# Decode attention: V loads moved from ACT's queue to SP's, with semaphores shared to make room

## The chip, the cores and the metric

The kernel runs on one core of a Trainium2 chip. The metric is the device time of one execution in microseconds (us). The core has five engines that run side by side, each with its own instruction stream: PE (matrix products; PEld is its loading of the stationary operand), DVE (vector), ACT (activations), POOL and SP. Sixteen DMA engines move data between HBM and the on-chip memory SBUF; an engine's instruction starts a transfer, and the transfer then runs by itself. PSUM is the memory into which PE writes its products.

The engines know of each other through semaphores only: an instruction, or a transfer when it lands, raises a semaphore, and an engine waits until it has reached a value. Raising by a transfer is by 16.

## What is computed

One token is decoded for two sequences. There are 32 heads of 128 values; the cache of each sequence and head holds 8192 keys and as many values. All of K and V (64 blocks of 2 MB each) is read once.

```python
xn = _layernorm(x)                                   # x: [2, 1, 512]
q  = (xn @ wq) as [2, 32 heads, 1, 128]
scores = einsum("bhqd,bhkd->bhqk", q, k_cache) * 128 ** -0.5   # k_cache: [2, 32, 8192, 128]
p  = softmax(scores)
o  = einsum("bhqk,bhkd->bhqd", p, v_cache)
return x + o.reshape(2, 1, 4096) @ wo + relu(xn @ w1) @ w2
```

Data is bf16. The program reads 280.5 MB from HBM, nearly all of it K and V.

## The kernel before

**Pairs.** The 64 blocks (sequence and head) are taken two at a time: 32 pairs. Partitions 0 to 63 hold one block of the pair and 64 to 127 the other. A pair's K is one tile of 128 x 16384 bf16, 4 MB, and so is its V. There are two buffers for K (`ks`) and two for V (`vs`), `R = 2`, used in turn. So K of pair t + 2 may be loaded once the K of pair t has been used, and V of pair t + 1 once the V of pair t - 1 has been used.

**One step of PE.** For every pair PE runs `step`. It waits for K of the pair (`dK`), then goes through 16 groups of 8 slices: group e is transposed into a PSUM tile (`transposes`, line 286), copied by DVE or ACT into SBUF (`kcopy`, line 413; the groups of `ON_ACT` go to ACT, the others to DVE), and multiplied with q (`scores`, line 293), two groups behind the transposes. Then come the products of the *preceding* pair's weights with its V (`weighted`, line 306): PE waits for V in `values` only here, more than half way into the step. In between, DVE finds the maximum (lines 467 and 472) and ACT makes the exponentials (line 530). At the end of the step the result is copied out by ACT in `out_copy` (line 518).

So step n uses K of pair n - 1 from its start, and V of pair n - 2 from its second half.

**Semaphores of the groups.** Each group has one for "transposed" (`pT[e]`) and one for "copied" (`kR[e]`), 16 of each; each rises by one in every pair, and the engines wait for the number of the pair, n, which they hold in a register and count up by one.

**Who issues the loads.** SP issues the start (wq into the second V buffer, w1, w2, K of pairs 0 and 1, V of pair 0), and then each K of pair t + 2 when the last group of pair t has been transposed (line 161, after a wait for `pT[NG - 1]`). ACT issues V of pair t + 1 at the end of its own work on pair t (line 548), after `out_copy`, which has waited for `sW`, the end of the products with V of pair t - 1. The two engines have a DMA queue each: in the profile q1 is SP's and q10 ACT's.

**The end.** V of the last pair is loaded by SP in two halves (line 183) when its buffer is free, and after it wo in five pieces (line 188: 14, 7, 6, 3 and 2 of 32 slices) into the place where w1 and w2 were. After the last step PE sums the denominators (line 361) and adds the other branch (line 364), does the products of the last pair with the two halves of V (line 306 again, 128 products), brings the result into the layout that wo needs (lines 379 and 384, with copies of DVE between), and multiplies by wo (line 398, 128 products), waiting for each piece of wo as it comes to it. Two copies, a transpose and the store (line 190) end the program.

**ACT's loop.** ACT's pairs run in a loop of 15 turns of two pairs, and the last two pairs are written out behind it, because no V is issued there.

Of the kernel before, what the change touches and what calls it, by code (L numbers as in the profile page):

```python
# [11 lines left out]
R = 2  # L12
EG = 8
NG = 16
REP = 32
ON_ACT = (0, 3, 5, 8, 11, 13)


@with_exitstack
def kernel(  # L20
# [12 lines left out]
    nc = tc.nc  # L33
    P = 128
# [12 lines left out]
    NP = N // 2  # L47
# [21 lines left out]
    def sem(name):  # L69
        return tc.alloc_semaphore(name)  # L70
# [58 lines left out]
    dW2 = sem("dW2")  # L129
    dK = [sem(f"dK{i}") for i in range(R)]  # L130
    dV = [sem(f"dV{i}") for i in range(R)]
    dH = [sem(f"dH{i}") for i in range(2)]
    dW = [sem(f"dWo{i}") for i in range(5)]
    sG, sI, sQ, sQ1 = sem("sG"), sem("sI"), sem("sQ"), sem("sQ1")
    sV, sA, sE = sem("sV"), sem("sA"), sem("sE")
    sS, sT, sB, sW = sem("sS"), sem("sT"), sem("sB"), sem("sW")
    pT = [sem(f"pT{e}") for e in range(NG)]
    kR = [sem(f"kR{e}") for e in range(NG)]
    sM, sX, sP, sO, sN = sem("sM"), sem("sX"), sem("sP"), sem("sO"), sem("sN")
    sH, sF, sZ = sem("sH"), sem("sF"), sem("sZ")  # L140

# [3 lines left out]
    wo_v = A_wo.rearrange("(p j) n -> p j n", j=WJ)  # L145
    cuts = (0, 14, 21, 27, 30, WJ)
    NC = len(cuts) - 1
    qp = ot[0][0:QG * Bsz, :]
    tpq = tp[1][:].rearrange("p g k -> p (g k)")[:, 0:N].rearrange(
        "p (l c) -> p l c", l=QH  # L150
# [9 lines left out]
    def load_k(t):  # L160
        nc.sync.dma_start(ks[t % R][:], K_all[t * P:(t + 1) * P, :]).then_inc(dK[t % R], 16)

    def load_v(t):
        nc.sync.dma_start(vs[t % R][:], V_all[t * P:(t + 1) * P, :]).then_inc(dV[t % R], 16)
# [5 lines left out]
    @(lambda f: f(nc.sync))  # L170
    def _(sp):
        sp.dma_start(w1_sb, B_w1.rearrange("(p kt) f -> p kt f", kt=KT)).then_inc(dW1, 16)  # L172
        sp.dma_start(w2_sb, B_w2.rearrange("(p j) n -> p j n", j=FJ)).then_inc(dW2, 16)  # L173
        load_k(0)
        load_k(1)
        load_v(0)
        for t in range(NP - 2):
            sp.wait_ge(pT[NG - 1], t + 1)
            load_k(t + R)
        sp.wait_ge(sW, NP - 1)  # L180
        for i in range(2):
            sl = slice(i * SLOT // 2, (i + 1) * SLOT // 2)
            sp.dma_start(
                vs[(NP - 1) % R][:, sl], V_all[(NP - 1) * P:NP * P, sl]
            ).then_inc(dH[i], 16)
        for c in range(NC):
            sl = slice(cuts[c], cuts[c + 1])
            sp.dma_start(wo_sb[:, sl, :], wo_v[:, sl, :]).then_inc(dW[c], 16)
        sp.wait_ge(sE, 1)
        sp.dma_start(  # L190
            out.rearrange("b s (c p) -> (b s c) p", p=P), osb[:]
        ).then_inc(dO, 16)


    @(lambda f: f(nc.gpsimd))
    def _(g):
# [34 lines left out]
    def _(pe):  # L231
# [51 lines left out]
        def transposes(r, e):  # L283
            for i in range(EG):
                kk = e * EG + i
                t = pe.transpose(tp[e % 4][:, i, :], ks[r][:, kk * Dh:(kk + 1) * Dh], identb[:])  # L286
            t.then_inc(pT[e], 1)

        def scores(r, e, n):
            pe.wait_ge(kR[e], n)  # L290
            for i in range(EG):
                kk = e * EG + i
                t = pe.matmul(  # L293
                    Sc[r][:, 2 * kk:2 * kk + 2 * REP],
                    lhsT=kT[e % 4][:, i, :],
                    rhs=rep(q2[r][:]),
                    start=True,
                    stop=True,
                )
            if e == NG - 1:  # L300
                t.then_inc(sS, 1)
# [17 lines left out]
            pe.wait_ge(sO, n)  # L319
            pe.wait_ge(dV[r], n16)  # L320

        def step(r, n, n16):


            pe.wait_ge(dK[r], n16)
            pe.wait_ge(sQ1, n)
            for e in range(NG):
                transposes(r, e)
                if e >= 2:
                    scores(r, e - 2, n)  # L330
            v = 1 - r
            values(v, n, n16)
            weighted(v, 0)
            scores(r, NG - 2, n)
            weighted(v, 1)
            scores(r, NG - 1, n)
            for e in range(2, NG):
                weighted(v, e)
                if e == 5:
                    pe.wait_ge(sM, n)  # L340
                    pe.transpose(tr_of(r), mcol[r][:], identb[:]).then_inc(sT, 1)  # L341
                if e == 8:
                    pe.wait_ge(sX, n)
                    pe.matmul(  # L344
                        bc_of(r), lhsT=onesb[:], rhs=mx[r][:], start=True, stop=True
                    ).then_inc(sB, 1)

        reg = nc.alloc_register(mybir.EngineType.PE, "pairno")
        pe.reg_mov(reg, 0)
        with pe.Fori(16, 16 * (NP // R) + 1, 16) as n16:  # L350
            for r in range(R):
                pe.reg_add(reg, reg, 1)
                step(r, reg, n16)

        pe.wait_ge(sP, NP + 1)
        pe.wait_ge(sO, NP + 1)
# [12 lines left out]
                stop=False,  # L369
            )  # L370
        for i in range(2):
            pe.wait_ge(dH[i], 16)
            for e in range(i * NG // 2, (i + 1) * NG // 2):
                weighted(1, e)

# [16 lines left out]

        pe.wait_ge(sV, 105)
        for c in range(NC):
            pe.wait_ge(dW[c], 16)
            for j in range(cuts[c], cuts[c + 1]):
                for k in range(KT):
                    t = pe.matmul(  # L398
                        fin[:, k, :],
                        lhsT=wo_sb[:, j, k * P:(k + 1) * P],  # L400
                        rhs=OX[:, j, :],
                        start=False,
                        stop=(j == WJ - 1 and k == KT - 1),
                    )
# [3 lines left out]
            tp[1][0:Bsz * KT, 0, :], yT[:].rearrange("p b c -> p (b c)"), identb[:]  # L408
        ).then_inc(sH, 1)

    def kcopy(eng, e):
        fn = eng.copy if e in ON_ACT else eng.tensor_copy
        fn(kT[e % 4][:], tp[e % 4][:]).then_inc(kR[e], 1)  # L413


    @(lambda f: f(nc.vector))
    def _(v):
# [38 lines left out]
        v.wait_ge(sF, 3)  # L456
        v.tensor_tensor(out=ys[:], in0=y, in1=xsb[:], op=ALU.add).then_inc(sF, 1)

        def pair(i, n):
            for e in range(NG):  # L460
                if e not in ON_ACT:
                    v.wait_ge(pT[e], n)
                    kcopy(v, e)
            v.wait_ge(sS, n)
            for u in range(2):
                half = slice(u * HP, (u + 1) * HP)
                m = v.tensor_reduce(  # L467
                    out=mcol[i][half, :], in_=S_of(i)[half, :, u], axis=AX.X, op=ALU.max
                )
            m.then_inc(sM, 1)  # L470
            v.wait_ge(sT, n)
            v.tensor_reduce(  # L472
                out=mx[i][:], in_=tr_of(i).rearrange("o (u m) -> o u m", u=2),
                axis=AX.X, op=ALU.max, negate=True,
            ).then_inc(sX, 1)

        reg = nc.alloc_register(mybir.EngineType.DVE, "pairno_v")
        v.reg_mov(reg, 0)
        with v.Fori(0, NP // R):
            for r in range(R):  # L480
                v.reg_add(reg, reg, 1)
                pair(r, reg)

        v.wait_ge(sH, 1)
        v.reciprocal(out=RD[:], in_=Sc[0][:, 0:N]).then_inc(sV, 1)
# [22 lines left out]
    @(lambda f: f(nc.scalar))  # L508
    def _(a):
        a.wait_ge(sV, 3)  # L510
        a.activation(
            out=rstd[:], in_=mv[:, 1:2], func=ACTF.Sqrt, bias=eps_t[:Bsz], scale=1.0
        ).then_inc(sA, 1)


        def out_copy(r, n, c):
            a.wait_ge(sW, n)
            a.copy(OTf[:, bass.ds(c, 2)], ot[r][:, 0:2]).then_inc(sO, 1)  # L518

        def pair(i, n, t):  # L520
            for e in range(NG):
                if e in ON_ACT:
                    a.wait_ge(pT[e], n)
                    kcopy(a, e)
            a.wait_ge(sB, n)
            a.copy(nm[i][:], bc_of(i)).then_inc(sN, 1)  # L526
            a.wait_ge(sN, n)
            for u in range(2):
                half = slice(u * HP, (u + 1) * HP)
                x = a.activation(  # L530
                    out=prm[i][half, :, u],
                    in_=S_of(i)[half, :, u],
                    func=ACTF.Exp,
                    bias=nm[i][half, u:u + 1],
                    scale=1.0,
                    accum_out=RS[half, bass.ds(t, 1)],
                )
            x.then_inc(sP, 1)
            out_copy(1 - i, n, t * 2)

        a.copy(nm[0][:, 0:1], eps_t[:]).then_inc(sO, 1)
        reg = nc.alloc_register(mybir.EngineType.Activation, "pairno_a")
        a.reg_mov(reg, 0)
        with a.Fori(0, NP // R - 1) as tr:
            for r in range(R):
                a.reg_add(reg, reg, 1)
                pair(r, reg, tr * R + r)
                a.dma_start(  # L548
                    vs[1 - r][:], V_all[bass.ds((tr * R + r + 1) * P, P), :]
                ).then_inc(dV[1 - r], 16)  # L550
        for r in range(R):
            a.reg_add(reg, reg, 1)
            pair(r, reg, NP - R + r)
# [1 line left out]
_INS = ['A_x', 'A_k_cache', 'A_v_cache', 'A_wq', 'A_wo', 'B_x', 'B_w1', 'B_w2']  # L555
_OUTS = [((2, 1, 512), 'bfloat16')]
# [25 lines left out]
```

## Time and profile before

| what | value |
| --- | --- |
| time, median of 3 runs | 665.18 us (665.15 to 665.19) |
| the profiled execution's own time | 665.18 us |
| its span, first to last instruction | 663.1 us |
| PE busy | 562.3 us (85%) |
| DVE busy | 253.3 us (38%) |
| ACT busy | 254.5 us (38%) |
| read from HBM | 280.50 MB, 423 GB/s over the span |
| mean granted clock of PE | 0.941 |

The span is what the profile shows; 2.1 us of the time lie around it. All rows below are of this one execution, and times in them count from the start of the span.

How rows are read. A group or timeline row names start or total in us, the line of the kernel, the engine, the operation, what it writes and reads, and how often. In brackets at the end of a timeline row is how long the engine was idle before it and what released it. SPq and ACTq are the parts of SP and ACT that issue transfers; a row of theirs is the issue, not the transfer. The list of DMA issues has the size of one and the median time from issue to landing. In rows for stretches of time there are the start and end, the length, the busy time of each engine, the granted clock, the mean busy share of the DMA engines and the rate in GB/s.

### The profile page before, as it was taken

How to read it: one execution, taken by the hardware profiler on the slowest of the kernel's cores; microseconds unless marked ns; L12 is line 12 of the kernel's file. 1: busy time of each engine (PE TensorE's matmuls, PEld its weight loads, DVE VectorE, ACT ScalarE, POOL GpSimd, SP SyncE). 2: the span in 40 equal slices, each digit the busy share in tenths (PEclk: the TensorE clock that was granted, in tenths of full speed). 3: DMA queues.
4: the chain of work that ended last, by engine and by line, in shares of the span. 5: the costliest groups of instructions: out<-in, count | busy, mean ns of one | idle time of the engine just before them, and what ended most of it. 6: DMA issues, size and time to landing. Idle time of an engine off the chain costs nothing.

```text
span 663.1 us, 26912 instructions
## 1 busy us (share of the span) xinstructions
PE 562.3 (85%) x12737; PEld 538.2 (81%) x12737; DVE 253.3 (38%) x436; ACT 254.5 (38%) x402; POOL 8.9 (1%) x46
## 2 busy tenths in 40 slices
PE   2998798887988788898887899788789987887987
PEld 0488798887988788898887889788789887887986
DVE  1144244343443334344343444434334443343441
ACT  1043344343444334344343434434343353433430
POOL 1000000000000000000000000000000000000000
PEclk9799899899989889998898999889899898899989
DMA  8999999999999999999999999999999999999994
GB/s 361 438 431 435 424 435 434 425 435 433 427 435 435 423 439 427 431 439 427 431 439 427 431 437 429 431 435 429 433 435 427 433 437 423 437 433 427 435 420 170
DMA packets 10542, 280.66 MB, mean 423 GB/s; under 512 B 1186, under 2 KB 1188, under 8 KB 1700
## 3 DMA queue, kind: packets, MB, share of 16 engines
q1 hardware_dynamic: 6208, 154.67, 54.4%
q10 hardware_dynamic: 4324, 125.83, 44.1%
q8 instruction: 9, 0.15, 0.1%
q14 instruction: 1, 0.01, 0.0%
HBM read 280.50 MB, written 0.00 MB: 423 GB/s over the span
## 4 chain that ended last, share of the span: by engine, by line
DMA 61%; PE 35%; ACT 2%; issue 1%; ACTq 0%; SPq 0%; DVE 0%
DMA ks<-in_A_k_cache_dram 61%; PE tp L286 20%; PE Sc L293 10%; PE ot L306 3%; ACT kT L413 1%; PE ot L398 1%; ACT L413 0%; ACTq L548 0%; PE ot L364 0%; PE Sc L361 0%; PE Sc L341 0%; SPq L173 0%; PE Sc L344 0%; SPq L172 0%; SPq L166 0%
## 5 line engine op out<-in xcount | busy, mean ns | idle before, releaser
L286 PE MATMUL tp<-identb,ks 128*128 128x128 bf16 x4096 | 326.0, 229 | 70.8 <-DMA ks<-in_A_k_cache_dram 70.8
L413 DVE COPY kT<-tp 128x1024 bf16<-128x1024 bf16 x320 | 219.9, 691 | 330.9 <-PE tp L286 330.7
L286 PEld LDWEIGHTS tp<-identb,ks 128*128 128x128 bf16 x4096 | 257.2, 103 | 74.7 <-DMA ks<-in_A_k_cache_dram 74.7
L413 ACT COPY kT<-tp 128x1024 bf16<-128x1024 bf16 x192 | 194.3, 1012 | 233.6 <-PE tp L286 233.5
L293 PE MATMUL Sc<-q,kT 128*128 128x64 bf16 x4096 | 217.7, 196 | 7.4 <-ACT kT L413 6.6
L293 PEld LDWEIGHTS Sc<-q,kT 128*128 128x128 bf16 x4096 | 179.5, 100 | 10.7 <-ACT kT L413 9.7
L306 PE MATMUL ot<-prm,vs 128*128 128x64 bf16 x4224 | 156.1, 192 | 5.0 <-issue 5.0
L306 PEld LDWEIGHTS ot<-prm,vs 128*128 128x128 bf16 x4224 | 139.0, 97 | 7.9 <-issue 5.2
L526 ACT COPY nm<-Sc 128x2 f32<-128x2 f32 x32 | 5.1, 160 | 118.1 <-PE Sc L344 118.1
L530 ACT ACTIVATE prm<-Sc,nm 64x128 bf16<-64x128 f32 x64 | 25.6, 400 | 4.1
L467 DVE TENSOR_REDUCE mcol<-Sc 64x1 bf16<-64x128 f32 x64 | 18.6, 291 | 18.3 <-PE Sc L293 17.8
L413 ACT ACT_TABLE_LOAD x15 | 19.2, 1283 | 9.3 <-issue 9.3
L241 PE MATMUL ot<-vs,xz 128*16 128x512 bf16 x32 | 9.4, 467 | 8.8 <-DMA vs<-in_A_wq_dram 8.8
L518 ACT COPY OTf<-ot 128x2 f32 (+1 forms) x32 | 5.1, 160 | 27.8 <-PE ot L306 27.8
L472 DVE TENSOR_REDUCE mx<-Sc 1x2 bf16<-1x128 bf16 x32 | 8.9, 279 | 16.9 <-PE Sc L341 16.9
L241 PEld LDWEIGHTS ot<-vs,xz 128*16 128x16 bf16 x32 | 3.3, 105 | 14.6 <-issue 12.3
L226 POOL COPY q<-qb 128x2 bf16<-128x2 bf16 x32 | 5.8, 184 | 595.2 <-PE Sc L293 572.3
L530 ACT ACTIVATION_READ_ACCUMULATOR prm<-Sc,nm (+1 forms) x64 | 11.8, 185 | 0.0
L443 DVE TENSOR_SCALAR qs<-ot 16x512 bf16<-16x512 f32 x1 | 0.7, 679 | 18.1 <-PE ot L241 18.1
L341 PE MATMUL Sc<-identb,mcol 128*1 128x128 bf16 x32 | 7.0, 217 | 0.0
L271 PE MATMUL Sc<-w_sb,hT 128*2 128x512 bf16 x14 | 5.8, 600 | 0.1
L344 PE MATMUL Sc<-mx,onesb 1*128 1x2 bf16 x32 | 5.5, 172 | 0.0
(56 smaller groups left out, 36.4 us busy)
## 6 DMA issues: line engine op xcount, KB each, us to landing
ks<-in_A_k_cache_dram SPq DMA_DIRECT2D x32, 4096.0 KB, 26.7
vs<-in_A_v_cache_dram ACTq DMA_DIRECT2D x30, 4096.0 KB, 28.6
vs<-in_A_wq_dram SPq DMA_DIRECT2D x1, 4096.0 KB, 12.4
vs<-in_A_v_cache_dram SPq DMA_DIRECT2D x1, 4096.0 KB, 49.1
vs<-in_A_v_cache_dram SPq DMA_DIRECT2D x2, 2048.0 KB, 13.0
w_sb<-in_B_w_dram SPq DMA_DIRECT2D x2, 1792.0 KB, 18.1
w_sb<-in_A_wo_dram SPq DMA_DIRECT2D x1, 1792.0 KB, 19.1
w_sb<-in_A_wo_dram SPq DMA_DIRECT2D x1, 896.0 KB, 18.6
```

The lines of the kernel that those rows point to most:

```text
L226: g.tensor_copy(q2[t % R][:], qb[:, 2 * t:2 * t + 2]).then_inc(sQ1, 1)
L241: i = pe.matmul(qp, lhsT=xz[:, kt, Z - g * Bsz:Z - g * Bsz + QG * Bsz], rhs=vs[1][:, (kt * QG + g) * 512:(kt * QG + g + 1) * 512], start=( ...
L271: i = pe.matmul(y, lhsT=hT[:, j, :], rhs=w2_sb[:, j, :], start=(j == 0), stop=(j == FJ - 1),)
L286: t = pe.transpose(tp[e % 4][:, i, :], ks[r][:, kk * Dh:(kk + 1) * Dh], identb[:])
L293: t = pe.matmul(Sc[r][:, 2 * kk:2 * kk + 2 * REP], lhsT=kT[e % 4][:, i, :], rhs=rep(q2[r][:]), start=True, stop=True,)
L306: t = pe.matmul(ot[r][:, 0:2 * REP], lhsT=vs[r][:, kk * Dh:(kk + 1) * Dh], rhs=rep(prm[r][:, kk, :]), start=(kk == 0), stop=(kk == KB - 1),)
L341: pe.transpose(tr_of(r), mcol[r][:], identb[:]).then_inc(sT, 1)
L398: t = pe.matmul(fin[:, k, :], lhsT=wo_sb[:, j, k * P:(k + 1) * P], rhs=OX[:, j, :], start=False, stop=(j == WJ - 1 and k == KT - 1),)
L413: fn(kT[e % 4][:], tp[e % 4][:]).then_inc(kR[e], 1)
L467: m = v.tensor_reduce(out=mcol[i][half, :], in_=S_of(i)[half, :, u], axis=AX.X, op=ALU.max)
L472: v.tensor_reduce(out=mx[i][:], in_=tr_of(i).rearrange("o (u m) -> o u m", u=2), axis=AX.X, op=ALU.max, negate=True,).then_inc(sX, 1)
L530: x = a.activation(out=prm[i][half, :, u], in_=S_of(i)[half, :, u], func=ACTF.Exp, bias=nm[i][half, u:u + 1], scale=1.0, accum_out=RS[half ...
```

## The change

- V of pairs 1 to 30 is issued by SP, in the loop that issues K: after K of pair t + 2, SP waits for the end of the products with V of pair t - 1 (`sW`), and issues V of pair t + 1.
- ACT issues no V, and its loop takes all 32 pairs.
- Groups e and e + 8 share one semaphore for transposes and one for copies. A semaphore so rises twice in every pair, and the engines wait for 2n - 1 for the first of the two groups and 2n for the second. Three registers count n, 2n - 1 and 2n, on PE, DVE and ACT.
- The two halves of the last V use the semaphores of the loads of w1 and w2, and the first piece of wo that of the load of x; the waits ask for 32 there.
- In all 47 semaphores are named in place of 66.

```diff
-ON_ACT = (0, 3, 5, 8, 11, 13)
+ON_ACT = (0, 3, 5)
...
-    dH = [sem(f"dH{i}") for i in range(2)]
-    dW = [sem(f"dWo{i}") for i in range(5)]
...
-    pT = [sem(f"pT{e}") for e in range(NG)]
-    kR = [sem(f"kR{e}") for e in range(NG)]
+    HG = NG // 2
+    pT = [sem(f"pT{e}") for e in range(HG)]
+    kR = [sem(f"kR{e}") for e in range(HG)]
...
+    NL = 16 * (NP // R)
+    last = [(dW1, 32), (dW2, 32)]
+    piece = [(dX, 32)] + [(sem(f"dWo{c}"), 16) for c in range(1, NC)]
...
         for t in range(NP - 2):
-            sp.wait_ge(pT[NG - 1], t + 1)
+            sp.wait_ge(pT[HG - 1], 2 * (t + 1))
             load_k(t + R)
+            sp.wait_ge(sW, t + 1)
+            load_v(t + 1)
...
-            ).then_inc(dH[i], 16)
+            ).then_inc(last[i][0], 16)
...
-            sp.dma_start(wo_sb[:, sl, :], wo_v[:, sl, :]).then_inc(dW[c], 16)
+            sp.dma_start(wo_sb[:, sl, :], wo_v[:, sl, :]).then_inc(piece[c][0], 16)
...
+    def counters(eng, kind):
+        regs = [nc.alloc_register(kind, f"count{i}_{kind.name}") for i in range(3)]
+        eng.reg_mov(regs[0], 0)
+        eng.reg_mov(regs[2], 0)
+        return regs[0], regs[1:]
+
+    def advance(eng, n, h):
+        eng.reg_add(n, n, 1)
+        eng.reg_add(h[0], h[1], 1)
+        eng.reg_add(h[1], h[1], 2)
...
-            t.then_inc(pT[e], 1)
-
-        def scores(r, e, n):
-            pe.wait_ge(kR[e], n)
+            t.then_inc(pT[e % HG], 1)
+
+        def scores(r, e, h):
+            pe.wait_ge(kR[e % HG], h[e // HG])
...
-            pe.wait_ge(dH[i], 16)
+            pe.wait_ge(*last[i])
...
-            pe.wait_ge(dW[c], 16)
+            pe.wait_ge(*piece[c])
...
-    def kcopy(eng, e):
-        fn = eng.copy if e in ON_ACT else eng.tensor_copy
-        fn(kT[e % 4][:], tp[e % 4][:]).then_inc(kR[e], 1)
+    def kcopies(eng, act, h):
+        fn = eng.copy if act else eng.tensor_copy
+        for e in range(NG):
+            if (e % HG in ON_ACT) == act:
+                eng.wait_ge(pT[e % HG], h[e // HG])
+                fn(kT[e % 4][:], tp[e % 4][:]).then_inc(kR[e % HG], 1)
...
-        with a.Fori(0, NP // R - 1) as tr:
+        reg, h = counters(a, mybir.EngineType.Activation)
+        with a.Fori(0, NP // R) as tr:
             for r in range(R):
-                a.reg_add(reg, reg, 1)
-                pair(r, reg, tr * R + r)
-                a.dma_start(
-                    vs[1 - r][:], V_all[bass.ds((tr * R + r + 1) * P, P), :]
-                ).then_inc(dV[1 - r], 16)
-        for r in range(R):
-            a.reg_add(reg, reg, 1)
-            pair(r, reg, NP - R + r)
+                advance(a, reg, h)
+                pair(r, reg, h, tr * R + r)
```

The same groups as before go to ACT (0, 3, 5, 8, 11 and 13), as `ON_ACT` is now read modulo 8.

More of the change, by code (lines that the diff above doesn't have):

```diff
@@ L320, in values, with step @@
             pe.wait_ge(dV[r], n16)
-        def step(r, n, n16):
+        def step(r, n, h, n16):
             pe.wait_ge(dK[r], n16)
@@ L329, in step @@
                 if e >= 2:
-                    scores(r, e - 2, n)
+                    scores(r, e - 2, h)
             v = 1 - r
@@ L333, in step @@
             weighted(v, 0)
-            scores(r, NG - 2, n)
+            scores(r, NG - 2, h)
             weighted(v, 1)
-            scores(r, NG - 1, n)
+            scores(r, NG - 1, h)
             for e in range(2, NG):
@@ L346, in step @@
                     ).then_inc(sB, 1)
-        reg = nc.alloc_register(mybir.EngineType.PE, "pairno")
-        pe.reg_mov(reg, 0)
-        with pe.Fori(16, 16 * (NP // R) + 1, 16) as n16:
+        reg, h = counters(pe, mybir.EngineType.PE)
+        with pe.Fori(16, NL + 1, 16) as n16:
             for r in range(R):
-                pe.reg_add(reg, reg, 1)
-                step(r, reg, n16)
+                advance(pe, reg, h)
+                step(r, reg, h, n16)
         pe.wait_ge(sP, NP + 1)
@@ L457, in _, with pair @@
         v.tensor_tensor(out=ys[:], in0=y, in1=xsb[:], op=ALU.add).then_inc(sF, 1)
[L459 to L463, printed above, removed]
+        def pair(i, n, h):
+            kcopies(v, False, h)
             v.wait_ge(sS, n)
@@ L475, in pair @@
             ).then_inc(sX, 1)
-        reg = nc.alloc_register(mybir.EngineType.DVE, "pairno_v")
-        v.reg_mov(reg, 0)
+        reg, h = counters(v, mybir.EngineType.DVE)
         with v.Fori(0, NP // R):
             for r in range(R):
-                v.reg_add(reg, reg, 1)
-                pair(r, reg)
+                advance(v, reg, h)
+                pair(r, reg, h)
         v.wait_ge(sH, 1)
@@ L518, in out_copy, with pair @@
             a.copy(OTf[:, bass.ds(c, 2)], ot[r][:, 0:2]).then_inc(sO, 1)
[L520 to L524, printed above, removed]
+        def pair(i, n, h, t):
+            kcopies(a, True, h)
             a.wait_ge(sB, n)
@@ L541, in _ @@
         a.copy(nm[0][:, 0:1], eps_t[:]).then_inc(sO, 1)
-        reg = nc.alloc_register(mybir.EngineType.Activation, "pairno_a")
-        a.reg_mov(reg, 0)
-        with a.Fori(0, NP // R - 1) as tr:
+        reg, h = counters(a, mybir.EngineType.Activation)
+        with a.Fori(0, NP // R) as tr:
             for r in range(R):
-                a.reg_add(reg, reg, 1)
-                pair(r, reg, tr * R + r)
-                a.dma_start(
-                    vs[1 - r][:], V_all[bass.ds((tr * R + r + 1) * P, P), :]
-                ).then_inc(dV[1 - r], 16)
-        for r in range(R):
-            a.reg_add(reg, reg, 1)
-            pair(r, reg, NP - R + r)
+                advance(a, reg, h)
+                pair(r, reg, h, tr * R + r)
 _INS = ['A_x', 'A_k_cache', 'A_v_cache', 'A_wq', 'A_wo', 'B_x', 'B_w1', 'B_w2']
```

## The prediction

> **What bounds the kernel now.** I read the slices first, then the queues, the chain of waits, the waits of PE for K, and last the end of the span in order of time. The page:
>
> ```profile
> span 663.1 us, 26912 instructions
> DMA  8999999999999999999999999999999999999994
> GB/s 361 438 431 435 424 435 434 425 435 433 427 435 435 423 439 427 431 439 427 431 439 427 431 437 429 431 435 429 433 435 427 433 437 423 437 433 427 435 420 170
> q1 hardware_dynamic: 6208, 154.67, 54.4%
> q10 hardware_dynamic: 4324, 125.83, 44.1%
> DMA 61%; PE 35%; ACT 2%; issue 1%; ACTq 0%; SPq 0%; DVE 0%
> L286 PE MATMUL tp<-identb,ks 128*128 128x128 bf16 x4096 | 326.0, 229 | 70.8 <-DMA ks<-in_A_k_cache_dram 70.8
> ```
>
> The reader is to see that the DMA engines are full in every slice but the first and the last, that two queues (SP's q1, ACT's q10) share them, and that PE waits 70.8 us in all for K, in 29 waits by the table of waits: 2.4 us each. The program is bound by transfers. The last slice is the exception: DMA falls to 170 GB/s there, so something else sets the very end. The end, from the timelines of SP, ACT and PE and from the DMA issues of short stretches:
>
> ```profile
> 592.92 1.29 PE L286 MATMUL tp<-identb,ks 128*128 128x128 bf16 x20 [2.13 <-DMA ks<-in_A_k_cache_dram]
> 603.86 0.33 SPq L161 DMA_DIRECT2D ks<-in_A_k_cache_dram  x1
> 609.22 0.34 ACTq L548 DMA_DIRECT2D vs<-in_A_v_cache_dram  x1
> 612.37 2.74 PE L286 MATMUL tp<-identb,ks 128*128 128x128 bf16 x24 [3.43 <-DMA ks<-in_A_k_cache_dram]
> 631.79 1.98 PE L286 MATMUL tp<-identb,ks 128*128 128x128 bf16 x24 [2.29 <-DMA ks<-in_A_k_cache_dram]
> 643.98 0.41 PE L306 MATMUL ot<-prm,vs 128*128 128x64 bf16 x8
> 647.12 1.89 PE L306 MATMUL ot<-prm,vs 128*128 128x64 bf16 x56
> 630.38 6.09 SPq L188 DMA_DIRECT2D w_sb<-in_A_wo_dram  x5
> 650.82 4.08 PE L306 MATMUL ot<-prm,vs 128*128 128x64 bf16 x128
> 656.42 3.36 PE L398 MATMUL ot<-OX,w_sb 128*128 128x2 bf16 x128 [0.32 <-DVE OX L499]
> ...
> ks<-in_A_k_cache_dram SPq DMA_DIRECT2D x1, 4096.0 KB, 27.9
> vs<-in_A_v_cache_dram ACTq DMA_DIRECT2D x1, 4096.0 KB, 27.4
> w_sb<-in_A_wo_dram SPq DMA_DIRECT2D x1, 256.0 KB, 19.1
> ```
>
> The last K (pair 31, issued at 603.86) lands at 603.86 + 27.9 = 631.8, and PE starts on it at once. From there PE runs to 659.78 (656.42 + 3.36) with no wait for a transfer. The last piece of wo was issued near 636.04 (the five issues together: 630.38 + 6.09, less one issue of 0.43) and lands at 636.04 + 19.1 = 655.1, before PE has begun to read wo at 656.42. So in steady state transfers set the pace, but the end is set by when the last K lands, plus 28 us of PE, not by the last transfer.
>
> **Why the last K is late.** K 31 and V 30 are in flight together on two queues. V 30 lands at 609.22 + 27.4 = 636.6, 4.9 us after K 31, though it is needed 12.2 us after it (643.98 - 631.79). The same in steady state: V 29, issued at 591.07 and 28.5 us under way, lands at 619.6, 7.2 us after K 30 at 612.37. Bandwidth that K waits for goes into V, which has time.
>
> **The change, part by part.** *V from SP, behind K.* V of pair t+1 now comes after K of pair t+2 on one queue, in exactly the order of need. One transfer of 4.194 MB takes 9.71 us at 432 GB/s, the rate of 300 to 600 us:
>
> ```profile
> 5.00:20.00 15.00, 6.53 (x20) 2.29 (x21) 0.00 (x0) 0.00 (x0) 0.00 (x0) 1.00 1.00 430
> 300.00:600.00 300.00, 259.07 (x5939) 252.99 (x5940) 119.81 (x201) 122.83 (x192) 2.76 (x15) 0.94 1.00 432
> ```
>
> The last columns are DMA share and GB/s; from 5 to 20 us only SP's queue carries bulk data, later both do. The rate is the same, so I leave all bytes ahead of V 31 to finish when they do now: its first half lands at 629.53 + 10.7 = 640.3. Counting back in the new order: V 30 lands at 640.3 - 4.85 = 635.4, K 31 at 635.4 - 9.71 = 625.7. That is 6.1 us earlier.
>
> PE's step follows at that distance: 17.2 us of work (631.79 to 649.01) against 19.42 between two Ks (2 x 9.71), so it keeps pace with 2.2 us in hand. It wants V 11 us (603.9 less 592.92, the shortest step that I saw) to 12.2 us after K; V lands 9.71 after. Hence the first wo product could begin at 656.42 - 6.1 = 650.3 and the last end at 653.7. Now wo is late next: its last piece stays at 655.1, and behind it stand 2 of 32 slices, 8 matmuls of 3.36/128 = 0.026 us, 0.2 us. New end of PE: 655.1 + 0.1 (a landing to PE's start, rounded up) + 0.2 = 655.4, against 659.78: **4.4 us less**. What follows, 663.1 - 659.78 = 3.3 us (two copies, a transpose, the store, the end), stays. The span becomes 658.7.
>
> Does the queue ever run dry? K of pair t+2 is issued 11 to 12 us after K of pair t lands, when K t+1 has 7 to 8 us to go and V t its 9.7 behind it. V t+1 is issued at the end of the step, 17 us after, with 12 us of transfers ahead of it. SP's waits cannot hold each other up: transposes, end of step, transposes, end of step is the order in which PE makes them. Early, steps last 18 to 20 us and K 2 comes at 62.3 (V 0 at 52.6 by the page, plus 9.7), K 4 at 101; the trace has PE waiting regularly from about 102 us on, so PE is caught up by pair 7 or so.
>
> *ACT loses per pair* one DMA issue of 0.34 us with register work of 0.09 (60 and 29 ns), and V is released by PE's last product, not after ACT's copy of 0.16 us. V so goes out 0.3 us earlier, into a queue with 12 us ahead of it: nothing. *The ACT loop takes 16 turns in place of 15 and two pairs written out*: one more table load of 1.28 us, as at each loop top. It falls between the end of a step and the next K, 2.2 us; without that cover, 1.3 us once. *Shared semaphores*: as many waits and signals as before, on values that rise in the same order; two register additions more per pair on PE, DVE and ACT. No row has them on PE; the nearest is ACT's register work, 60 ns, so 0 to 0.12 us a pair. PE's wait of 2.2 us for K hides it; if that were gone, 32 x 0.12 = 3.8 us. *47 semaphores in place of 66*: at most 19/66 of the 2.1 us between the store's issue (660.58 + 0.37) and the end, 0.6 us of gain; I take 0, no row separates it. *Late loads on semaphores of early ones*: the early loads are long waited for; nothing.
>
> *The price of one queue.* Bounds: the nearest row gives 430 against 432 GB/s, 0.46% of some 560 us, 2.6 us of loss; on the other side the two long stretches that the windows give, 431 (100 to 300 us) and 432, differ by 0.23%, 1.3 us of gain if one queue had the better of them. By landings, K 1 and V 0 on SP's queue alone took 52.6 - 32.9 = 19.7 us (the first K lands at 2.34 + 30.54 by the chain of waits), 0.3 more than two at 9.71; instruction fetches fell in that stretch too, so I take 0.
>
> The Trainium skill (DMA: Bandwidth & Descriptors, Anatomy of one DMA) fits a fixed 2.0 us to every DMA beside its bytes. If one queue paid that between transfers, 60 of them would cost an estimated 120 us; the 19.7 us above for two transfers leaves no room for it. The same page (Issuing engines are not separate DMA queues) says that several issuing engines save only issue time. By it alone the move is worth nothing and the time stays 665.2; the trace agrees on rate, but it shows order to count, by the 4.9 and 7.2 us between K and V.
>
> **The rivals.** *No change.* K 31 lands where it does, because the engines would serve the two queues in some order that favours K already, or because something other than K starts the last step. For it: PE's idle time is only 2.3 us there. Against: V 30 lands 4.9 us after K 31 where a queue in order has 9.7. Time 665.
>
> *Slower: gaps on the single queue.* q10 no longer fills what q1 leaves open at the seam of two transfers. Price by the landings above: 0.3 us a pair, 30 pairs, 9 us; less 4.4: 669.8 (at 0.23, by an unrounded 19.66, it would be 667.7). It eats the gain from 4.4/30 = 0.15 us a pair on. For it: that row. Against: 430 to 432 GB/s, and DMA share 1.00 in both stretches.
>
> *V too late.* V misses the 11 us after K by skew between engines; PE then stalls where it waits for K now. Up to 2.2 us a step is free, and the transfers go on; at the end, wo is last still. Time 661 to 662: a variant of the forecast.
>
> **How the numbers follow.** The profiled execution is the median run itself: 665.18 with a span of 663.1, 2.1 outside. Forecast 658.7 + 2.1 = **660.8 us**, chance 0.80 with late V in it; no change 0.08; gaps 0.12. The range: above, 2.6 us of the rate row give 663.4; below, the 0.6 us of semaphores and the 1.3 us of a better rate give 658.9; I stop at 659.2, as both in full are unlikely together. Measurement tells 0.2% (1.3 us) from no change. Faster: the forecast and a little of gaps that are smaller than their price, 0.82; same 0.07; slower 0.11.
>
> **What would show it.** q10 empty but for x; K to landing about 27 to 28 us still, as the period is the same, but PE's last step starts near 626 in place of 631.79, and PE waits for wo at the end, on line 398's counterpart. The last landing near 655, GB/s near 432 in mid-span. The forecast is wrong if the last wo piece lands after 657, if GB/s falls below 430, or if the last K stays near 631.

## The result and the profile after

The changed kernel takes **660.75 us** (median of 6 runs, 660.47 to 660.88) against 665.18 us before in the same session (665.14 to 666.03): a ratio of 0.993, with a 95% interval of 0.9917 to 0.9942. The profiled execution took 660.75 us with a span of 658.7 us, 2.05 us outside it. Forecast were 660.8 and 658.7.

On the page of the kernel before, the chain by line, and the DMA issues of K and V with their median time to landing, read:

```profile
DMA ks<-in_A_k_cache_dram 61%; PE tp L286 20%; PE Sc L293 10%; PE ot L306 3%; ACT kT L413 1%; PE ot L398 1%; ACT L413 0%; ACTq L548 0%; PE ot L364 0%; PE Sc L361 0%; PE Sc L341 0%; SPq L173 0%; PE Sc L344 0%; SPq L172 0%; SPq L166 0%
...
ks<-in_A_k_cache_dram SPq DMA_DIRECT2D x32, 4096.0 KB, 26.7
vs<-in_A_v_cache_dram ACTq DMA_DIRECT2D x30, 4096.0 KB, 28.6
```

The page of the changed kernel, lines that answer to those of before (the queues, the chain that ended last, the wait of PE for K, and the DMA issues with their median time to landing):

```profile
span 658.7 us, 26862 instructions
...
q1 hardware_dynamic: 10528, 280.50, 99.1%
...
q10 hardware_dynamic: 4, 0.00, 0.0%
...
DMA ks<-in_A_k_cache_dram 54%; PE tp L302 22%; PE Sc L309 11%; PE ot L322 4%; DMA w_sb<-in_A_wo_dram 4%; ACT kT L431 1%; ACT L431 1%; SPq L193 0%; PE Sc L357 0%; SPq L188 0%; PE Sc L360 0%; SPq L176 0%; SPq L175 0%; SPq L169 0%; PE ot L413 
...
L302 PE MATMUL tp<-identb,ks 128*128 128x128 bf16 x4096 | 323.3, 228 | 68.7 <-DMA ks<-in_A_k_cache_dram 68.7
...
ks<-in_A_k_cache_dram SPq DMA_DIRECT2D x32, 4096.0 KB, 26.7
vs<-in_A_v_cache_dram SPq DMA_DIRECT2D x31, 4096.0 KB, 31.3
```

q10 has only x left. PE waits for K about as long in all as before (68.7 against 70.8 us), and K is under way for 26.7 us as before: the pace of a pair has not changed, it is the transfers' own. What is new is in the chain, where wo stands now (28.9 us of the last piece, 4%); in the line of before it does not appear. V takes longer, 31.3 in place of 28.6, and nobody waits for it.

The end, in the timeline of PE in the changed kernel (start, duration, and in brackets how long PE was idle and what released it):

```profile
606.19 2.14 PE L302 MATMUL tp<-identb,ks 128*128 128x128 bf16 x24 [2.38 <-DMA ks<-in_A_k_cache_dram]
625.62 1.51 PE L302 MATMUL tp<-identb,ks 128*128 128x128 bf16 x24 [2.22 <-DMA ks<-in_A_k_cache_dram]
...
643.54 5.54 PE L322 MATMUL ot<-prm,vs 128*128 128x64 bf16 x128
...
653.51 1.42 PE L413 MATMUL ot<-OX,w_sb 128*128 128x2 bf16 x36 [0.55 <-DMA w_sb<-in_A_wo_dram]
655.08 0.37 PE L413 MATMUL ot<-OX,w_sb 128*128 128x2 bf16 x8 [0.15 <-DMA w_sb<-in_A_wo_dram]
```

The step of the last pair begins at 625.62 in place of 631.79. Then PE catches up with the transfers: the last 8 products wait for the last piece of wo, issued at 626.18 and 28.9 us under way, so landed at 655.1, as before. They end at 655.45, 4.3 us sooner than the last product of before (659.78).

The rate, in two stretches of the changed kernel (busy time of each engine, granted clock, DMA share, GB/s):

```profile
100.00:300.00 200.00, 175.33 (x4099) 170.75 (x4097) 80.93 (x138) 84.45 (x135) 2.06 (x11) 0.95 1.00 431
300.00:600.00 300.00, 259.11 (x6008) 253.16 (x6005) 121.48 (x204) 122.56 (x191) 2.80 (x16) 0.94 1.00 432
```

One queue carries 431 and 432 GB/s over these 500 us, what two carried.

### The profile page after: what moved, and what is told of

Same layout as the page of the kernel before. It is cut to its first block, busy times and chain, and to the rows that moved or that the text cites. A ratio compares the mean times of both kernels' runs of the same rounds, so it can differ in the third digit from the quotient of the medians.

```text
span 658.7 us, 26862 instructions
## 1 busy us (share of the span) xinstructions
PE 559.4 (85%) x12737; PEld 536.4 (81%) x12737; DVE 253.2 (38%) x436; ACT 255.9 (39%) x403; POOL 9.0 (1%) x46
## 4 chain that ended last, share of the span: by engine, by line
DMA 58%; PE 37%; ACT 2%; issue 1%; SPq 1%; ACTq 0%; DVE 0%
DMA ks<-in_A_k_cache_dram 54%; PE tp L302 22%; PE Sc L309 11%; PE ot L322 4%; DMA w_sb<-in_A_wo_dram 4%; ACT kT L431 1%; ACT L431 1%; SPq L193 0%; PE Sc L357 0%; SPq L188 0%; PE Sc L360 0%; SPq L176 0%; SPq L175 0%; SPq L169 0%; PE ot L413 0%
## 5 line engine op out<-in xcount | busy, mean ns | idle before, releaser
L302 PE MATMUL tp<-identb,ks 128*128 128x128 bf16 x4096 | 323.3, 228 | 68.7 <-DMA ks<-in_A_k_cache_dram 68.7
L322 PEld LDWEIGHTS ot<-prm,vs 128*128 128x128 bf16 x4224 | 140.5, 98 | 7.9 <-issue 5.2
L532 ACT COPY OTf<-ot 128x2 f32 x32 | 5.1, 160 | 27.7 <-PE ot L322 27.7
L541 ACT ACTIVATION_READ_ACCUMULATOR prm<-Sc,nm x64 | 11.8, 185 | 0.0
L413 PE MATMUL ot<-OX,w_sb 128*128 128x2 bf16 x128 | 4.0, 166 | 1.2 <-DMA w_sb<-in_A_wo_dram 0.7
## 6 DMA issues: line engine op xcount, KB each, us to landing
ks<-in_A_k_cache_dram SPq DMA_DIRECT2D x32, 4096.0 KB, 26.7
vs<-in_A_v_cache_dram SPq DMA_DIRECT2D x31, 4096.0 KB, 31.3
```

Of the source, the lines that this page charges most:

```text
L322: t = pe.matmul(ot[r][:, 0:2 * REP], lhsT=vs[r][:, kk * Dh:(kk + 1) * Dh], rhs=rep(prm[r][:, kk, :]), start=(kk == 0), stop=(kk == KB - 1),)
L541: x = a.activation(out=prm[i][half, :, u], in_=S_of(i)[half, :, u], func=ACTF.Exp, bias=nm[i][half, u:u + 1], scale=1.0, accum_out=RS[half ...
```

## The experiments

The theory is that the *order* in which the bytes come makes the difference, that it makes it only at the end, and that the last piece of wo then sets the end. Rivals: the shared semaphores or the registers bring something; each of the 30 moved loads brings its thirtieth; it is the single queue, or ACT freed of its issues, that helps. Each kernel ran beside runs of the kernel before, and its ratio is to those.

### The two parts of the change, each alone

V from SP in the kernel before, all 66 semaphores kept:

```diff
             sp.wait_ge(pT[NG - 1], t + 1)
             load_k(t + R)
+            sp.wait_ge(sW, t + 1)
+            load_v(t + 1)
...
-        with a.Fori(0, NP // R - 1) as tr:
+        with a.Fori(0, NP // R) as tr:
...
-                a.dma_start(
-                    vs[1 - r][:], V_all[bass.ds((tr * R + r + 1) * P, P), :]
-                ).then_inc(dV[1 - r], 16)
-        for r in range(R):
-            a.reg_add(reg, reg, 1)
-            pair(r, reg, NP - R + r)
```

> The kernel before with one part of the change: V of pairs 1 to 30 issued by SP behind K; all 66 semaphores stay. Theory (order of the transfers): the last K lands near 625.6 in place of 631.7, PE is held at the end by the last piece of wo, 660.8 us. Rival (the shared semaphores or their registers carry part of the 4.4 us): above 661.5, up to 665.2.

Measured: 660.86 us (660.73 to 661.07), ratio 0.9918 (0.9902 to 0.9933). The whole gain is there.

The opposite, the changed kernel with V from ACT:

```diff
             load_k(t + R)
-            sp.wait_ge(sW, t + 1)
-            load_v(t + 1)
...
-        with a.Fori(0, NP // R) as tr:
+        with a.Fori(0, NP // R - 1) as tr:
             for r in range(R):
                 advance(a, reg, h)
                 pair(r, reg, h, tr * R + r)
+                a.dma_start(
+                    vs[1 - r][:], V_all[bass.ds((tr * R + r + 1) * P, P), :]
+                ).then_inc(dV[1 - r], 16)
+        for r in range(R):
+            advance(a, reg, h)
+            pair(r, reg, h, NP - R + r)
```

> The changed kernel with V of pairs 1 to 30 issued by ACT again: what is left of the change is the sharing of semaphores, the second and third register and the late loads on early semaphores. Theory: all of it lies under PE's wait for K, 665.2 us (664.6 if fewer semaphores shorten the end, the bound of 0.6). Rival: the registers cost PE up to 0.12 us a pair, up to 669.

Measured: 665.88 us (664.71 to 667.87), ratio 0.9995 (0.9982 to 1.0008): no change that can be told. What the sharing, the registers and the late loads on early semaphores cost or bring lies between a gain of 1.2 us and a loss of 0.5.

### One load moved, or one left behind

In the kernel before, V of pair 30 alone goes to SP:

```diff
         for t in range(NP - 2):
             sp.wait_ge(pT[NG - 1], t + 1)
             load_k(t + R)
+        sp.wait_ge(sW, NP - 2)
+        load_v(NP - 2)
...
+            if t + 1 < NP - 2:
+                a.dma_start(
+                    vs[1 - t % R][:], V_all[(t + 1) * P:(t + 2) * P, :]
+                ).then_inc(dV[1 - t % R], 16)
```

The second part is ACT's: its loop ends one turn earlier, and behind the loop it issues V of pair 29 alone.

> The kernel before with one load moved: V of pair 30 is issued by SP behind K of pair 31; V of pairs 1 to 29 stays on ACT's queue. Theory (only what shares the bandwidth with the last K counts, since every earlier byte is moved by then in either order): the last K lands at 625.6 as with all 30 moved, 660.8 us. Rival (each moved load brings its thirtieth): 665.18 - 4.4/30 = 665.0 us.

Measured: 662.14 us (660.95 to 665.56), ratio 0.9943 (0.9921 to 0.9966). One load of 30 brings most of the gain, so the thirtieth is out; but 1.3 us are missing from what I expected. The timelines of SP and PE in this kernel show where they went:

```profile
604.75 0.33 SPq L161 DMA_DIRECT2D ks<-in_A_k_cache_dram  x1
609.86 0.33 SPq L164 DMA_DIRECT2D vs<-in_A_v_cache_dram  x1
...
613.23 2.74 PE L288 MATMUL tp<-identb,ks 128*128 128x128 bf16 x24 [3.41 <-DMA ks<-in_A_k_cache_dram]
630.17 1.50 PE L288 MATMUL tp<-identb,ks 128*128 128x128 bf16 x24
```

The last K was issued at 604.75 and 20.9 us under way: it landed at 625.7, as expected. But K of pair 30 had come at 613.2 in the old order, and PE was in that step until 630.2, 4.5 us after the landing; some 1.5 us of slack that PE has before wo (see below) are gone first, and the rest of the delay shows at the end. I had followed the transfer and not the engine that takes it. So two loads must be moved. V of pairs 29 and 30 to SP, the others left on ACT:

```diff
             load_k(t + R)
+            if t + 1 > NP - 4:
+                sp.wait_ge(sW, t + 1)
+                load_v(t + 1)
...
-        with a.Fori(0, NP // R - 1) as tr:
+        with a.Fori(0, NP // R - 2) as tr:
...
-        for r in range(R):
+        for t in range(NP - 2 * R, NP):
```

> The kernel before with two loads moved: V of pairs 29 and 30 are issued by SP behind K of pairs 30 and 31; V of pairs 1 to 28 stays on ACT's queue. With V 30 alone the last K landed at 625.68, but PE was in the step of pair 30 until 630.17, as that had begun with K 30 at 613.2. Theory: K 30 lands near 606.2, PE takes it after the step of pair 29 near 609.5, ends that step near 626 and goes on with the last K at once; the last wo piece at 655.1 sets the end again, 660.8 to 661.2 us. Rival (each moved load brings its thirtieth): 664.9 us.

Measured: 660.9 us (660.77 to 663.53; five of the six runs lie below 661), ratio 0.9929 (0.991 to 0.9948), the same as with all 30 within what can be told. PE in this kernel:

```profile
609.63 1.50 PE L289 MATMUL tp<-identb,ks 128*128 128x128 bf16 x24
625.57 1.51 PE L289 MATMUL tp<-identb,ks 128*128 128x128 bf16 x24
...
653.42 1.96 PE L401 MATMUL ot<-OX,w_sb 128*128 128x2 bf16 x44 [0.96 <-DMA w_sb<-in_A_wo_dram]
```

The steps of pairs 30 and 31 begin at 609.63 and 625.57, and PE waits for wo at the end. Now the opposite: all V from SP but the last of the 30 (ACT's loop ends two turns earlier, and the pairs behind it are taken one by one).

```diff
             load_k(t + R)
-            sp.wait_ge(sW, t + 1)
-            load_v(t + 1)
+            if t + 1 < NP - 2:
+                sp.wait_ge(sW, t + 1)
+                load_v(t + 1)
...
+            if t + 1 == NP - 2:
+                a.dma_start(
+                    vs[1 - t % R][:], V_all[(t + 1) * P:(t + 2) * P, :]
+                ).then_inc(dV[1 - t % R], 16)
```

> The changed kernel with one load put back: V of pair 30 is issued by ACT, the 29 others by SP. Theory: V 30 starts at once beside K 30, V 29 and K 31, which stand in SP's queue, and takes half the bandwidth; K 31 lands when all four are through, near 635.3, and PE's 28 us and the 3.3 behind them end at 666.6: 668.7 us, slower than before though 29 of 30 loads are moved. V 29 comes late too, near 625.6, which stalls PE some 5 us inside its step. Rival (each moved load brings its thirtieth): 660.9 us.

Measured: 669.55 us (668.58 to 670.13), ratio 1.0045 (1.0027 to 1.0062): slower than before with 29 of 30 loads moved. PE in this kernel:

```profile
624.38 0.59 PE L323 MATMUL ot<-prm,vs 128*128 128x64 bf16 x8 [5.95 <-DMA vs<-in_A_v_cache_dram]
...
635.22 2.74 PE L303 MATMUL tp<-identb,ks 128*128 128x128 bf16 x24 [4.65 <-DMA ks<-in_A_k_cache_dram]
```

The stray V has the other queue to itself. Issued at 603.7 and 23.3 us under way, it lands at 627.0: ahead of K 31, which was issued 5 us earlier and comes at 635.2 (635.3 expected). V 29 lands before it, but it shares the bandwidth too and is 41.0 us under way in place of 31.3, so PE stalls 5.95 us (5 expected) inside its step. The time is 0.9 us above the 668.7 expected; the granted clock in the last step was 0.82 here and 0.91 in the next run, which has the same last landing.

### The order alone, on one queue

In the changed kernel only the last K changes places with the V ahead of which it stood:

```diff
-            load_k(t + R)
+            if t < NP - 3:
+                load_k(t + R)
             sp.wait_ge(sW, t + 1)
             load_v(t + 1)
+            if t == NP - 3:
+                load_k(t + R)
```

> The changed kernel with one swap: K of pair 31 is issued behind V of pair 30, both at the end of the step of pair 29, when V 29 and the end of K 30 still stand in the queue, so that it does not run dry. One queue, the same bytes. Theory (order): the last K lands where V 30 landed, near 635.3; PE ends 28 us later and the span 3.3 after that: 668.7 us. Rival (what helps is the single queue or ACT freed of its issues): 660.8 us.

Measured: 668.92 us (668.45 to 670.04), ratio 1.0043 (1.0025 to 1.0061). PE in this kernel:

```profile
635.23 2.74 PE L305 MATMUL tp<-identb,ks 128*128 128x128 bf16 x24 [13.12 <-DMA ks<-in_A_k_cache_dram]
```

The queue, the bytes and ACT's work are those of the changed kernel; one swap takes 8.2 us. V 30 and K 31 have exchanged their landings: V 30, issued at 604.0 and 21.5 us under way, lands at 625.5, where K 31 landed in the changed kernel, and K 31 three transfers of 9.71 behind the 606.1 of K 30. So it is the order.

The same swap in all pairs was tried before it:

```diff
             sp.wait_ge(pT[HG - 1], 2 * (t + 1))
-            load_k(t + R)
             sp.wait_ge(sW, t + 1)
             load_v(t + 1)
+            load_k(t + R)
```

> The changed kernel with the two issues of SP swapped: V of pair t + 1 is issued ahead of K of pair t + 2, both at the end of the step; one queue, the same bytes, the same semaphores. Theory (order): the last K lands where V 30 landed, near 635.3 in place of 625.6, PE ends 28 us later, 668.7 us, and up to 1 us more if the queue runs short early. Rival (one queue, or ACT freed of its issues, is what helps): 660.8 us.

Measured: 703.19 us (700.59 to 705.87), ratio 1.0561 (1.0518 to 1.0604). Slower as expected, but by 37 us against the kernel before, where 3.5 were worked out, so it can't stand as a test of the order. SP's issues and the rate in stretches of this kernel:

```profile
358.32 0.33 SPq L167 DMA_DIRECT2D vs<-in_A_v_cache_dram  x1
358.69 0.43 SPq L164 DMA_DIRECT2D ks<-in_A_k_cache_dram  x1
...
300.00:600.00 300.00, 252.58 (x5706) 247.40 (x5704) 116.02 (x194) 117.34 (x181) 2.80 (x15) 0.91 0.98 409
...
359.00:361.00 2.00, 0.59 (x11) 0.59 (x12) 0.00 (x0) 0.97 (x1) 0.00 (x0) 1.00 0.68 229
```

With both loads held until the end of the step, only one transfer was left in the queue at the issue, with some 2 us to go. Right after the issue at 358.32 the rate falls to 229 GB/s for 2 us. The packet records of the trace show two causes, over the issues between 100 and 610 us. Half a us after an issue of V, 4 of the 16 DMA engines on the average have no packet in flight (in the changed kernel none is without). And 197 of the 6391 packets of 32 KB took more than 1.6 us in place of 1.2, 182 of them within 4 us behind an issue of V (in the changed kernel 1 of 6721 did). So the queue runs dry at many pairs, and 432 GB/s become 409. For 280.5 MB that is 37 us more than in the changed kernel, or 1.2 us a pair; with the 8.2 us of the order it comes near the 42 us measured between the two. I had allowed for being up to 1 us short, early only. In the changed kernel K goes out some 5 us before V, and this does not happen: of the times to landing there, 26.7 us for K and 31.3 for V, 9.7 are the transfer's own, so 17 us of transfers stand ahead of a K at its issue and 22 ahead of a V. In last_k_behind_v V 30 had 12 us ahead of it at its issue, and nothing was lost.

### What sets the end now, and what a seam costs

The changed kernel with wo in one piece:

```diff
-    cuts = (0, 14, 21, 27, 30, WJ)
+    cuts = (0, WJ)
```

> The changed kernel with wo loaded in one piece in place of five. Theory (the end is set by the last landing of wo, with what is left to do behind it): all 128 products of 0.026 us stand behind the landing at 654.8 to 655.0, 3.4 us in place of 0.2; 663.7 to 664.0 us. Rival (PE is still what sets the end): its first wo product can begin near 650.3 anyway and the time stays near 660.8.

Measured: 664.29 us (664.16 to 664.88), ratio 0.997 (0.9959 to 0.9981), 3.5 us above the changed kernel. PE in this kernel:

```profile
654.97 3.55 PE L413 MATMUL ot<-OX,w_sb 128*128 128x2 bf16 x128 [3.72 <-DMA w_sb<-in_A_wo_dram]
```

PE waits 3.72 us for wo, and all 128 products stand behind the landing. The end is the last landing and what is left behind it. The time is 0.3 us above the expected range: the products took 3.55 us for 3.4, and from their end to the end of the span 3.8 us passed for 3.3, why is not known. By its trace the kernel before gained nothing from the pieces, as PE began with wo after the last had landed; now they carry 3.5 us.

The changed kernel with each K in two transfers of half a row:

```diff
+    dKb = [sem(f"dKb{i}") for i in range(R)]
...
-        nc.sync.dma_start(ks[t % R][:], K_all[t * P:(t + 1) * P, :]).then_inc(dK[t % R], 16)
+        for i, d in enumerate((dK, dKb)):
+            sl = slice(i * SLOT // 2, (i + 1) * SLOT // 2)
+            nc.sync.dma_start(
+                ks[t % R][:, sl], K_all[t * P:(t + 1) * P, sl]
+            ).then_inc(d[t % R], 16)
...
             pe.wait_ge(dK[r], n16)
+            pe.wait_ge(dKb[r], n16)
```

> The changed kernel with each K loaded as two transfers of half a row (16 KB runs in place of 32), two semaphores and two waits: 32 more seams between transfers on the one queue. Theory (no gap at a seam): only the shorter runs cost, by the records of the packets 2 x 0.611 against 1.213 us, 0.009 x 8 a K and engine, 0.07 us; 32 of them and as many 9 ns signals give 2.6 us, 663.4 us. Rival (a gap of 0.15 us or more at each seam): 668 us or more.

Measured: 663.23 us (663.12 to 663.45), ratio 0.996 (0.9942 to 0.9979): 2.5 us above the changed kernel for 32 more seams and runs half as long, as the records of the packets said (2.6). The run does not part the shorter packets from the seams. Even if all of it were laid on the seams it would be 0.08 us each; the rival's 0.15 is out.

## Why the prediction was right

**What bounds the kernel.** Right: the last K with PE's work behind it set the end of the kernel before. last_k_behind_v and all_but_last_v move that one landing to 635.2, and the time follows it to 668.9 and 669.6, where 668.7 was worked out.

**Counting back from V 31.** Right to 0.1 us. K 31 was put at 625.7 and PE began on it at 625.62. The base, that all bytes ahead of V 31 end when they did, holds too: its first half, issued at 623.44 and 16.7 us under way, lands at 640.1 (640.3 forecast), and V 30 at 603.85 + 31.4 = 635.3 (635.4).

**The end behind wo.** Right: 655.4 forecast for the last product, 655.45 measured, and 3.3 us behind it. Two terms were off in opposite directions and hid each other. The last step was taken at 17.2 us, and took 16.0; the products with the last V were taken at 4.1 us, and took 5.54, at a granted clock of 0.70 where it was 1.00 before. The first product with wo began at 650.60 against 650.3. Rows of the stretches, the kernel before first, then the changed one:

```profile
631.80:649.00 17.20, 17.20 (x386) 16.89 (x386) 7.77 (x13) 7.14 (x11) 0.00 (x0) 0.90 0.98 417
650.80:654.90 4.10, 4.10 (x129) 3.96 (x129) 0.00 (x0) 0.00 (x0) 0.00 (x0) 1.00 0.67 265
```

```profile
625.60:641.60 16.00, 15.76 (x386) 15.34 (x386) 7.69 (x13) 7.14 (x11) 0.00 (x0) 1.00 1.01 432
643.50:649.10 5.60, 5.59 (x129) 5.45 (x129) 0.00 (x0) 0.00 (x0) 0.00 (x0) 0.70 0.98 412
```

The clock (third number from the right) was low in the step before, in the products after. With 3.36 us of products from 650.60 on PE would have ended at 653.96, so it had 1.5 us in hand against wo, and neither showed.

**The queue never dry.** Right for this order, by the rate of 431 to 432 GB/s. The prediction gave V 12 us of transfers ahead of it at its issue. That left out K of pair t + 2, which SP issues 5 us earlier; the 31.3 us to landing show 22. The slip is on the safe side. That a full queue is a condition and not a matter of course is what v_before_k shows: with 2 us left at the issue it fails.

**One queue at no price.** Right. The landing row, 0.3 us a pair, which made the rival of 669.8, did not recur: K 30 and K 31 come 19.43 us apart (606.19 and 625.62), which is 2 x 9.71, and k_in_halves leaves at most 0.08 us a seam. The Trainium skill (DMA: Bandwidth & Descriptors, Anatomy of one DMA) gives its fixed 2.0 us by a fit to DMAs that were issued from GpSimd, which the prediction did not say; the loads here are issued by SP and ACT. In k_in_halves 32 more transfers cost 2.5 us in all, so no such cost is paid here between transfers that stand in a queue. What v_before_k lost when its queue ran dry was some 1.2 us a pair.

**Registers, semaphores, ACT's loop at nothing.** Right within what can be told: sems_alone has a ratio of 0.9995 (0.9982 to 1.0008) with registers and semaphores, and v_alone, with ACT's longer loop and none of the sharing, is within 0.11 us of the changed kernel. So the up to 0.6 us for fewer semaphores did not show beyond 0.11. ACT has one table load more, 16 in place of 15 on the pages, as forecast.

**The rivals.** *No change* is out by v_alone and last_two_v; *gaps* by k_in_halves. *V too late* did not come about: PE has no wait for V in the table of waits. The skill's sentence that issuing from several engines only saves issue time (same page, Issuing engines are not separate DMA queues) agrees with the rate, 431 to 432 GB/s with one queue and with two. The time changes all the same, by 5.4 us in v_alone. On two queues V 30 landed 4.8 us behind the last K (636.6 and 631.8); on one it lands 9.7 behind it (635.3 and 625.5), and K so much earlier.

**The size of the gain.** The 4.4 us were counted from one execution of the kernel before, of 665.18 us. In the sessions of v_alone and last_two_v the kernel before took 666.21 and 665.96 us, and the gain was 5.4 and 5.1 us. The time of the changed kernel is explained, and 4.4 us of the gain; the rest is that the kernel before was slower in those sessions, and its cause is open. That the gain came out at 4.4 in the first session is luck to that extent.

What the text did not say is that the gain is made in the last two pairs alone. It was implied by the sum, which counts only from the last K; last_v_alone, where I left out the step that PE must finish first, showed that two are needed.

## What to carry to other kernels

Where transfers are the bound, the sum of the bytes is fixed, and what can be won is at the end: find the last transfer behind which much work stands, and see that nothing that is needed later shares the bandwidth with it. Loads in the order of need on one queue do that; a second queue lets a later load pass, and may be worse than none if only one load is left on it. Keep enough in the queue at every issue (2 us of transfers were too little here; some 17 were enough at every K, and 12 the one time they were tried), and cut the load that comes last into pieces.

## What the runs showed of the hardware

- **The kernel before scatters more than the changed one.** In four sessions it gave 665.1 to 666.0, 664.0 to 667.4, 663.8 to 667.6 and 665.0 to 668.5 us. With all V on SP's queue, in the order of need, the times lie within 0.4 us (660.47 to 660.88, and 660.73 to 661.07 with the semaphores of before). Two things differ: the second queue, and that PE's work and not a landing sets the end. The other runs do not part them: last_k_behind_v, with one queue and PE's work at the end, gave 668.45 to 670.04, and last_two_v, with two queues and a landing at the end, 660.77 to 660.93 and once 663.53. A profiled execution of sems_alone that took 667.87 us shows where such a loss can lie: from 80 to 100 us its rate was 403 GB/s, and in the kernel before 431. That is 1.3 us of transfers, of the 2.8 us by which its last K was later (634.59 against 631.79). Why the rate falls in some executions only was not tried.

- **Equal steps of PE differ in granted clock.** A step of PE that begins without a wait (last_two_v, 609.63 to 625.57) took 15.9 us at a granted clock of 1.00; one that begins after 2.3 us of wait took 17.2 in the kernel before, at 0.90. But the step at 625.62 of the changed kernel began after a wait of 2.22 us too and took 16.0 at 1.00, so the wait alone does not decide. What does was not tried.

- **The first packets after a queue has run dry are slow.** Between 100 and 610 us of v_before_k 197 packets of 32 KB took 1.6 to 3.4 us, where 1.2 is the median; in the changed kernel, whose queue did not run dry there, one did.
